# Moving filter sums, modulation loads and late adds in a fused FFT and FFN kernel

## The chip, the cores and the metric

The kernel runs on one core of one Trainium2 chip. The metric is device time in microseconds (us) of that core. It was 255.58 us before the change (median of 3 runs, 255.17 to 255.83).

The engines are named as in the profile: PE is the matmul engine, PEld its weight loads, DVE the vector engine, ACT the scalar engine, POOL the general engine (GpSimd), SP the engine that issues most of the DMAs. PSUM is the memory that matmuls write.

## The reference, cut to what matters

```python
def _A_ref(x, w_r, w_i):                      # x: (1, 2048, 640)
    X = rfft2(x.astype(float32))              # over both axes
    X = X * (w_r + 1j * w_i)                  # the "filter"
    return irfft2(X, s=(S, D)).astype(bfloat16)

def _B_ref(x, w_gate, w_up, w_down):          # 640 -> 1728 -> 640
    return silu(x @ w_gate) * (x @ w_up) @ w_down

mod = (silu(c) @ w_mod).reshape(1, 6, 1, -1)  # six vectors of 640
sa, ca, ga, sb, cb, gb = ...
h = layernorm(x) * (1 + ca) + sa
x = x + ga * _A_ref(h, A_w_r, A_w_i)
h = layernorm(x) * (1 + cb) + sb
x = x + gb * _B_ref(h, B_w_gate, B_w_up, B_w_down)
```

All inputs are bfloat16. Each FFT is done as a chain of matmuls with tables, so the program has four parts: a first DFT with layernorm statistics (0 to 37 us), a loop over 21 groups of columns that multiplies by the filter (37 to 62 us, its beginning is called the join here), the inverse DFT with the second layernorm (to 85 us), and the FFN in three chunks of rows (85 us to the end).

## The kernel before: the parts that matter

Everything large is loaded by one DMA queue, which SP issues. This is its order around the join. `Wn` holds the filter, `Wv` the filter in flipped row order, which the kernel first writes to device memory and then reads back. `wm_r[:, :, 0]` holds the gate weights (`ga`), `wm_r[:, :, 1:3]` those of `sb` and `cb`.

```python
for i, w in ((0, A_w_i), (2, A_w_r)):
    nc.sync.dma_start(Wn[:, i, :, :], w.rearrange(...)[:, :, 0:NW])        # filter
nc.sync.dma_start(KS2, K_dram[:, 384:576])
# ...
for i in range(2):
    nc.sync.dma_start(Wv[:, 2 * i, :, :], Wflip[i][:])                     # flipped filter
nc.sync.dma_start(Ktab[:, 0:384], K_dram[:, 0:384])
nc.sync.dma_start(wm_r[:, :, 0, :], wm_m[:, :, 0, :])                      # gate weights
# ... later, at the join:
t2_dma(0); t2_dma(1); t2_dma(2)                                            # DMA transposes
nc.sync.dma_start(wm_r[:, :, 1:3, :], wm_m[:, :, 1:3, :])                  # shift and scale weights
t2_dma(3)
```

The filter products need the sum of the real and imaginary filter. `wsum` makes it in pieces, on DVE or on POOL. The last three lines run just before the join.

```python
def wsum(W, lo, hi, eng):
    # ... views of columns lo to hi of the three filter planes
    eng.tensor_tensor(v[1], v[2], v[0], ALU.add)
# ...
if t == 13:
    wsum(Wn, 48, 64, nc.vector)          # 512 elements per partition
else:                                    # t == 15
    wsum(Wn, 0, 48, nc.vector)           # 1536 elements
    wsum(Wn, 64, 81, nc.gpsimd)
```

The group loop: `stage_a` is the matmul, `prod` the product on DVE. For the first two groups the second half of the product was put off. `ga_mod` makes the gate broadcast with matmuls, and the inner loop of `stage_a` makes the modulation columns.

```python
def stage_a(g):
    # ... for each column l of the group: a matmul, and at the first one:
        for c5 in {NG - 8: (0,), NG - 7: (0,), NG - 6: (1,), NG - 5: (1, 2), NG - 4: (2,), NG - 3: (3,), NG - 2: (3, 4), NG - 1: (4,)}.get(g, ()):
            # ... five small matmuls with wm_r[:, k, 1 + g % 2]
    prod(g, PP, xps, 0)
    if g > 1:
        prod(g, PP, xps, 1)
    return PP, xps
# ...
t2_pe(0)
wsum(Wv, 48, 64, nc.vector)
t2_pe(1)
PX = [stage_a(0)]
t2_pe(2)
PX.append(stage_a(1))
t2_pe(3)
ga_mod(0, 6)
ga_mod(320, 7, range(3))
for g in range(2):
    PPs[g] = PX[g][0]
    prod(g, *PX[g], 1)
for g in range(NG + 1):
    sa_add(g + 4 if g > 0 else 0)
    if g in (0, 1, 4):
        wsum(Wv, *{0: (64, 81), 1: (0, 16), 4: (16, 48)}[g], nc.gpsimd)
    if g + 2 < NG:
        PPs[g + 2] = stage_a(g + 2)[0]
    if g == 0:
        ga_mod(320, 7, range(3, NC5))
    # ...
```

Before the FFN the transposed rows come by DMA (`ln2_tr`), and `ln2_mod(0)` multiplies them in five pieces, all on POOL. In the FFN, `down_pair` is the down projection of two row tiles. It copies partial results out of PSUM on ACT and adds them on POOL. `a_sum` makes the sums of the Strassen-like scheme that the down projection uses.

```python
cps_ = [rL.cut((2560, 10496, 0, 1280)[i], [320], F32) for i in range(4)]
# ... in down_pair:
nc.scalar.copy(cps_[0], X)
nc.gpsimd.tensor_tensor(xa[:, 0:320], xa[:, 0:320], cps_[0], ALU.add)
# ...
nc.scalar.copy(cps_[2], X)                     # PE needs the PSUM bank of X again
nc.gpsimd.tensor_tensor(xb[:, 320:640], xb[:, 320:640], cps_[1], ALU.add)
nc.gpsimd.tensor_tensor(xa[:, 320:640], xa[:, 320:640], cps_[2], ALU.add)
# ... at the end of the last chunk:
r1, r2, r3, r4 = (lambda q=q: a_sum(ATc, 0, q, slice(0, 6)) for q in range(4))
```

The bytes of `cps_[2]` (0 to 1280 of `rL`) are also an input of a DVE product of the gate and up stage, line 1062.

## Time and profile before

| | before |
|---|---|
| time, median of 3 | 255.58 us |
| profiled span | 254.3 us |
| granted clock | 1.00 |
| PE, DVE, ACT, POOL busy | 245.3, 212.0, 162.3, 77.4 us |

These two lines of the page give the span and the busy time of each engine:

```profile
span 254.3 us, 6460 instructions
...
PE 245.3 (96%) x2513; PEld 200.1 (79%) x2513; DVE 212.0 (83%) x517; ACT 162.3 (64%) x299; POOL 77.4 (30%) x123
```

PE is busy for 96% of the span, so by the page's count a change of order alone can return at most its idle 9 us. The list of waits tells where they lie. Each line of it names an engine and line that waited, what released it, the total, how many waits, and the longest. These are the larger PE waits before, apart from one of 1.0 us at the very start:

```profile
PE psum L897 <- ACT rL L919: 0.8, 2, 0.4
PE psum L570 <- DMA rM<-in_w_mod_dram: 0.7, 1, 0.7
PE psum L566 <- DVE rM L541: 0.6, 1, 0.6
PE psum L971 <- POOL rW L784: 0.4, 1, 0.4
PE psum L537 <- ACT rA L403: 0.4, 1, 0.4
PE psum L897 <- DVE rE L854: 0.3, 1, 0.3
```

L537, L566 and L570 are the join and the group loop, L971 is the first matmul behind the second layernorm, and L897 is the down projection of the FFN. The DVE timeline at the join is next. Its columns are start, duration, engine, line, operation, and output and input with the shape per partition; a count above x1 joins neighbours.

```profile
36.61 1.90 DVE L410 TENSOR_TENSOR rW<-rW 128x1536 bf16<-128x1536 bf16 x1
38.43 0.47 DVE L541 TENSOR_TENSOR rM<-psum,gb_bc 128x256 bf16<-128x256 bf16 x2
38.83 0.41 DVE L410 TENSOR_TENSOR rW<-rW 128x512 bf16<-128x512 bf16 x1
39.34 2.06 DVE L588 TENSOR_TENSOR rM<-psum,rW 128x384 bf16<-128x384 f32 x4
```

DVE has no pause here. The long sum takes 1.90 us, more than four times the 0.41 us of a sum of a third of its size, and the first product starts at 39.34.

The wait at L919 reads as follows. ACT holds the copy back until DVE has finished L1062, which reads the bytes that the copy writes, and PE waits for the copy:

```profile
177.26 1.00 DVE L1062 TENSOR_TENSOR rX<-rH,rL 128x512 bf16<-128x512 bf16 x1
...
178.35 0.42 ACT L919 COPY rL<-psum 128x320 f32<-128x320 f32 x1 [1.39 <-DVE rX L1062]
...
178.83 1.11 PE L897 MATMUL psum<-rE 128*128 128x320 f16 x7 [0.42 <-ACT rL L919]
```

At the end of the last chunk DVE makes sums while POOL adds:

```profile
244.96 0.75 DVE L854 TENSOR_TENSOR rE<-rX 128x128 f16<-128x128 bf16 x1
245.63 0.68 DVE L856 TENSOR_TENSOR rE<-rE,rX 128x768 f16<-128x768 f16 x2
246.24 1.35 DVE L860 TENSOR_TENSOR rE<-rX,rE 128x768 f16<-128x768 bf16 x2
247.51 1.38 DVE L858 TENSOR_TENSOR rE<-rX 128x768 f16<-128x768 bf16 x2
...
244.77 0.86 POOL L910 TENSOR_TENSOR rM<-rM,rL 128x320 f32<-128x320 f32 x1 [17.83 <-ACT rL L909]
246.62 0.88 POOL L920 TENSOR_TENSOR rM<-rM,rL 128x320 f32<-128x320 f32 x1 [0.99 <-ACT rL L916]
247.95 0.86 POOL L921 TENSOR_TENSOR rM<-rM,rL 128x320 f32<-128x320 f32 x1 [0.45 <-ACT rL L919]
```

The two pairs that overlap a POOL add in full (L860 and L858) take twice as long as the pair that hardly does (L856).

### The profile page before, as it was taken

How to read it: one execution, taken by the hardware profiler on the slowest of the kernel's cores; microseconds unless marked ns; L12 is line 12 of the kernel's file. 1: busy time of each engine (PE TensorE's matmuls, PEld its weight loads, DVE VectorE, ACT ScalarE, POOL GpSimd, SP SyncE). 2: the span in 40 equal slices, each digit the busy share in tenths (PEclk: the TensorE clock that was granted, in tenths of full speed). 3: DMA queues.
4: the chain of work that ended last, by engine and by line, in shares of the span. 5: the costliest groups of instructions: out<-in, count | busy, mean ns of one | idle time of the engine just before them, and what ended most of it. 6: DMA issues, size and time to landing. Idle time of an engine off the chain costs nothing.

```text
span 254.3 us, 6460 instructions
## 1 busy us (share of the span) xinstructions
PE 245.3 (96%) x2513; PEld 200.1 (79%) x2513; DVE 212.0 (83%) x517; ACT 162.3 (64%) x299; POOL 77.4 (30%) x123
## 2 busy tenths in 40 slices
PE   8999998989999999999999999999999999999994
PEld 3678868989789888688877778886678887679962
DVE  2889898978898997779997997879985888993895
ACT  3678757978788686778862577674357765235630
POOL 7487785954022804000003900002220000440021
PEclk9999999999999999999999999999999999999999
DMA  6999999999999899600005020004210000211001
GB/s 220 396 348 298 283 391 175 264 314 389 283 350 269 198 263 172 142 14 0 3 0 106 17 76 15 3 3 80 70 44 14 3 0 17 39 52 54 4 0 52
DMA packets 45760, 34.43 MB, mean 135 GB/s; under 512 B 21731, under 2 KB 42658, under 8 KB 45346
## 3 DMA queue, kind: packets, MB, share of 16 engines
q1 hardware_dynamic: 43936, 30.00, 42.5%
q0 software_dynamic: 1504, 3.95, 6.6%
q8 instruction: 19, 0.31, 0.5%
q10 hardware_dynamic: 290, 0.08, 0.1%
q14 instruction: 11, 0.09, 0.1%
HBM read 26.72 MB, written 4.72 MB: 124 GB/s over the span
## 4 chain that ended last, share of the span: by engine, by line
PE 69%; DVE 10%; DMA 7%; issue 5%; POOL 4%; SPq 2%; ACT 2%; ACTq 0%; DVEq 0%; POOLq 0%
PE psum L1013 31%; PE psum L897 14%; PE psum L983 8%; DMA rM<-in_w_mod_dram 3%; PE psum L877 3%; SPq L518 2%; DMA rW<-rL 2%; DMA rE<-tab_R 2%; PE psum L971 2%; PE psum L595 2%; PE psum L397 1%; PE psum L396 1%; POOL rW L784 1%; PE psum L317 1%; PE psum L314 1%
## 5 line engine op out<-in xcount | busy, mean ns | idle before, releaser
L1013 PEld LDWEIGHTS <-rW 128*128 128x128 bf16 (+1 forms) x528 | 46.9, 98 | 5.6 <-issue 0.2
L910 POOL TENSOR_TENSOR rM<-rM,rL 128x320 f32<-128x320 f32 x7 | 7.0, 1002 | 85.9 <-ACT rL L909 85.9
L1013 PE MATMUL psum<-rW 128*128 128x256 bf16 (+1 forms) x240 | 27.1, 259 | 0.0
L897 PEld LDWEIGHTS <-rE 128*128 128x128 f16 (+1 forms) x196 | 18.8, 97 | 10.2 <-issue 1.2
L897 PE MATMUL psum<-rE 128*128 128x320 f16 (+1 forms) x147 | 22.7, 299 | 1.3 <-ACT rL L919 0.8
L1013 PE MATMUL psum<-rY,rW 128*128 128x256 bf16 (+1 forms) x96 | 24.0, 259 | 0.0
L983 PE MATMUL psum<-rW 128*128 128x256 bf16 (+1 forms) x170 | 23.1, 291 | 0.0
L588 DVE TENSOR_TENSOR rM<-psum,rW 128x384 bf16<-128x384 f32 (+2 forms) x42 | 20.2, 544 | 3.0 <-PE psum L566 2.5
L983 PEld LDWEIGHTS <-rW 128*128 128x128 bf16 x170 | 16.6, 98 | 3.8
L1013 PEld LDWEIGHTS <-rE 128*128 128x128 f16 x192 | 17.3, 98 | 2.6 <-DVE rE L961 0.3
L1049 DVE TENSOR_TENSOR rH<-psum,rW 128x512 bf16<-128x512 f32 x21 | 14.5, 689 | 5.8 <-PE psum L1013 3.9
L897 PEld LDWEIGHTS <-rX 128*128 128x128 bf16 (+1 forms) x151 | 14.6, 97 | 5.4
L758 POOL TENSOR_TENSOR rstd<-rstd,mhalf 128x4 f32<-128x4 f32 (+2 forms) x4 | 4.7, 1186 | 45.9 <-ACT rL L919 38.1
L1045 ACT COPY rH<-psum 128x512 f32<-128x512 f32 x21 | 12.3, 585 | 9.8 <-PE psum L1013 7.9
L1067 DVE TENSOR_TENSOR rX<-rH,rL 128x512 bf16<-128x512 bf16 x21 | 8.9, 424 | 9.9 <-ACT rL L1065 9.8
L1052 ACT COPY rX<-psum 128x512 f32<-128x512 f32 x21 | 12.3, 587 | 6.5 <-PE psum L1013 6.5
L1053 DVE TENSOR_TENSOR rX<-psum,rX 128x512 f32<-128x512 f32 x21 | 14.4, 685 | 2.1 <-ACT rX L1052 1.9
L1039 ACT COPY rW<-psum 128x512 f32<-128x512 f32 x21 | 12.3, 585 | 6.0 <-PE psum L1013 6.0
L385 DVE SCALAR_TENSOR_TENSOR rE<-rE,mv,psum 128x648 bf16<-128x648 f32 (+1 forms) x17 | 14.2, 845 | 1.9 <-PE psum L317 1.5
L897 PE MATMUL psum<-rA,rX 128*128 128x320 bf16 (+1 forms) x98 | 15.6, 299 | 0.0
L1013 PE MATMUL psum<-rH,rW 128*128 128x256 f16 (+1 forms) x96 | 15.1, 259 | 0.1
L1013 PE MATMUL psum<-rE,rY 128*128 128x256 f16 (+1 forms) x96 | 15.1, 259 | 0.0
(195 smaller groups left out, 679.9 us busy)
## 6 DMA issues: line engine op xcount, KB each, us to landing
out_dram<-rA SPq DMA_DIRECT2D x31, 80.0 KB, 1.6
rM<-in_w_mod_dram SPq DMA_DIRECT2D x3, 800.0 KB, 9.7
rX<-in_A_x_dram SPq DMA_DIRECT2D x3, 640.0 KB, 7.0
rA<-in_B_w_down_dram SPq DMA_DIRECT2D x2, 960.0 KB, 10.7
rM<-in_w_mod_dram SPq DMA_DIRECT2D x1, 1600.0 KB, 7.9
rY<-in_B_w_gate_dram POOLq DMA_DIRECT2D x2, 768.0 KB, 6.9
rW<-in_B_w_gate_dram SPq DMA_DIRECT2D x2, 640.0 KB, 7.3
rW<-in_B_w_up_dram SPq DMA_DIRECT2D x2, 640.0 KB, 7.6
```

What stands on the lines that cost most here:

```text
L385: nc.vector.scalar_tensor_tensor(Zv[:, h], Cv[:, h], mv[:, t, 0:1], zps[:, h], ALU.mult, ALU.subtract)
L588: nc.vector.tensor_tensor(PP[:, :, hl], xv[:, :, hl], in1, ALU.mult)
L877: nc.tensor.matmul(pop, lhsT=ATc[rows(k), k, tl * 128:(tl + 1) * 128], rhs=Wd_sb[rows(k), k, 320 * h:320 * h + 320], start=(k == 0), stop= ...
L897: nc.tensor.matmul(o, lhsT=lhsT, rhs=rhs, start=start, stop=stop, skip_group_check=True)
L983: nc.tensor.matmul(gu[u], lhsT=Wgu[:, u, c5, ff * 128:(ff + 1) * 128], rhs=h2T[:, :, c5, :], start=(c5 == 0), stop=(c5 == NC5 - 1))
L1013: nc.tensor.matmul(o[:, f], lhsT=w, rhs=b, start=(start and f == 0 and i == 0), stop=(stop and f == F - 1 and i == len(ops) - 1), skip_gro ...
L1039: nc.scalar.copy(c0, X)
L1045: nc.scalar.copy(c2, X)
L1049: nc.vector.tensor_tensor(c11, Z, c0, ALU.add)
L1052: nc.scalar.copy(c3, X)
L1053: nc.vector.tensor_tensor(c22, Y, c3, ALU.add)
L1067: nc.vector.tensor_tensor(ato, v4(c11), v4(g21), ALU.mult)
```

## The change

The change has five parts, and its intent is to close the PE waits listed above.

1. Start: the statistics are split, so that the first scale of POOL (`gscale(0)`) no longer stands behind the second tile's statistics. POOL's broadcast copy (`sc_rep`) and some warm-up matmuls (`idle_pe`) move too; the cut below leaves them out.
2. Join: the gate weights are loaded before the flipped filter, and their matmuls fill holes of PE. The POOL sum beside DVE's long sum goes away and comes back in small pieces later. The product of the first two groups is no longer split. The modulation columns come two groups later.
3. Before the FFN: one of the five pieces goes from POOL to ACT.
4. FFN: `cps_[2]` moves to bytes that L1062 does not read, and `h_sums` changes its order.
5. Tail: the last chunk's three adds go from POOL to DVE, and a third of its sums is made earlier.

```diff
+    nc.sync.dma_start(wm_r[:, :, 0, :], wm_m[:, :, 0, :])      # ahead of the flipped filter
     nc.sync.dma_start(KS2, K_dram[:, 384:576])
# ... start: stats(t) split into bn(t), gram_stats(t) and rstd_of(tiles)
+        gscale(0)
         t1(1)
-        stats(1)
-        gscale(0)
+        bn(1)
+        rstd_of((1,))
# ... join
                     wsum(Wn, 0, 48, nc.vector)
-                    wsum(Wn, 64, 81, nc.gpsimd)
# ...
-                    for c5 in {NG - 8: (0,), NG - 7: (0,), NG - 6: (1,), NG - 5: (1, 2), ...
+                    for c5 in {NG - 6: (0, 1), NG - 5: (0, 1), NG - 4: (2, 3), NG - 3: (2,), NG - 2: (4,), NG - 1: (3, 4)}.get(g, ()):
# ...
             prod(g, PP, xps, 0)
-            if g > 1:
-                prod(g, PP, xps, 1)
+            prod(g, PP, xps, 1)
# ...
+        ga_mod(320, 5, range(3))
         t2_pe(0)
         wsum(Wv, 48, 64, nc.vector)
         t2_pe(1)
-        PX = [stage_a(0)]
+        ga_mod(320, 5, range(3, NC5))
+        PPs[0] = stage_a(0)
         t2_pe(2)
-        PX.append(stage_a(1))
         t2_pe(3)
-        ga_mod(0, 6)
-        ga_mod(320, 7, range(3))
-        ...
+        wsum(Wn, 80, 81, nc.gpsimd)
+        wsum(Wv, 80, 81, nc.gpsimd)
+        PPs[1] = stage_a(1)
+        ga_mod(0, 6, range(2))
         for g in range(NG + 1):
-            if g in (0, 1, 4):
-                wsum(Wv, *{0: (64, 81), 1: (0, 16), 4: (16, 48)}[g], nc.gpsimd)
+            for W, lo, hi in {0: ((Wv, 0, 16),), 1: ((Wv, 16, 32),), 3: ((Wv, 32, 48),), 11: ((Wn, 64, 80),), 13: ((Wv, 64, 80),)}.get(g, ()):
+                wsum(W, lo, hi, nc.gpsimd)
# ... before the FFN
-            if ci == 0:
+            if ci == 0 and c5 < 4:
                 nc.gpsimd.tensor_scalar(h2T[:, :, c5, :], ...)
# ... FFN
-    cps_ = [rL.cut((2560, 10496, 0, 1280)[i], [320], F32) for i in range(4)]
+    cps_ = [rL.cut((2560, 10496, 9216, 1280)[i], [320], F32) for i in range(4)]
# ... tail (three adds, and the sums)
+        add = (nc.vector if last else nc.gpsimd).tensor_tensor
-        nc.gpsimd.tensor_tensor(xa[:, 0:320], xa[:, 0:320], cps_[0], ALU.add)
+        add(xa[:, 0:320], xa[:, 0:320], cps_[0], ALU.add)
# ...
+            if n == 2 and p == 2:
+                for q in (0, 2, 1, 3):
+                    a_sum(ATc, 0, q, slice(0, 2))
# ...
-            r1, r2, r3, r4 = (lambda q=q: a_sum(ATc, 0, q, slice(0, 6)) for q in range(4))
+            r1, r2, r3, r4 = (lambda q=q: a_sum(ATc, 0, q, slice(2, 6)) for q in range(4))
```

More of the change, by code (lines that the diff above doesn't have):

```diff
@@ L277, in adaln_block_kernel @@
         nc.sync.dma_start(Wn[:, i, :, :], w.rearrange("(k2 k1) l -> k1 k2 l", k1=P)[:, :, 0:NW])
+    wm_m = wm_v[:, :, 2 * D:6 * D].rearrange("p k (i d) -> p k i d", i=4)
+    nc.sync.dma_start(wm_r[:, :, 0, :], wm_m[:, :, 0, :])
     nc.sync.dma_start(KS2, K_dram[:, 384:576])
-    wm_m = wm_v[:, :, 2 * D:6 * D].rearrange("p k (i d) -> p k i d", i=4)
     nc.vector.memset(ones[:], 1.0)
@@ L296, in idle_pe @@
                              start=True, stop=True)
-    idle_pe(6)
+    idle_pe(4)
     def mod_cols(ps_ap, w_ap, ks=range(NC5), w=1):
@@ L338, in t1, with bn, rstd_of @@
             hTs[t] = hT
-        def stats(t):
-            if t in BN:
-                for k in range(2):
-                    nc.vector.bn_stats(bn6a[:, k, :], x_sb[:, t, 320 * k:320 * k + 320])
-                nc.vector.bn_aggr(mv[:, t, :], bn6a[:])
-            else:
-                gram_stats(t)
-            if t % 2 == 1 or t == 0:
-                us = (t,) if t < 2 else (t - 1, t)
-                for u in us:
-                    if u in BN:
-                        nc.vector.tensor_scalar(vtmp[:, u:u + 1], mv[:, u, 1:2], EPS, float(D), ALU.add, ALU.mult)
-                for tt in ([slice(t - 1, t + 1)] if t not in BN and t - 1 not in BN else [slice(u, u + 1) for u in us if u not in BN]):
-                    nc.vector.scalar_tensor_tensor(vtmp[:, tt], mv[:, tt, 0], -float(D), mv[:, tt, 0], ALU.mult, ALU.mult)
-                    nc.vector.scalar_tensor_tensor(vtmp[:, tt], ssq[:, tt], EPS * D, vtmp[:, tt], ALU.add, ALU.add)
-                tt = slice(us[0], t + 1)
-                nc.gpsimd.tensor_tensor(rstd[:, tt], vtmp[:, tt], mhalf[:, 0:len(us)], ALU.pow)
+        def bn(t):
+            for k in range(2):
+                nc.vector.bn_stats(bn6a[:, k, :], x_sb[:, t, 320 * k:320 * k + 320])
+            nc.vector.bn_aggr(mv[:, t, :], bn6a[:])
+        def rstd_of(us):
+            bns = [u for u in us if u in BN]
+            for u in bns:
+                nc.vector.tensor_scalar(vtmp[:, u:u + 1], mv[:, u, 1:2], EPS, float(D), ALU.add, ALU.mult)
+            for tt in ([slice(u, u + 1) for u in us if u not in BN] if bns else [slice(us[0], us[-1] + 1)]):
+                nc.vector.scalar_tensor_tensor(vtmp[:, tt], mv[:, tt, 0], -float(D), mv[:, tt, 0], ALU.mult, ALU.mult)
+                nc.vector.scalar_tensor_tensor(vtmp[:, tt], ssq[:, tt], EPS * D, vtmp[:, tt], ALU.add, ALU.add)
+            tt = slice(us[0], us[-1] + 1)
+            nc.gpsimd.tensor_tensor(rstd[:, tt], vtmp[:, tt], mhalf[:, 0:len(us)], ALU.pow)
         def gram_stats(t):
@@ L414, in adaln_block_kernel @@
             nc.tensor.matmul(cps[:, k:k + 1], lhsT=c_row[0:1, k * 128:(k + 1) * 128], rhs=one11[:], start=True, stop=True)
-        idle_pe(3)
+        idle_pe(4)
         nc.scalar.activation(sc_f[:], cps, ACT.Silu)
@@ L419, in adaln_block_kernel @@
                                 op=ALU.add)
+        bn(0)
         for r in range(4):
@@ L423, in adaln_block_kernel @@
         nc.gpsimd.memset(SAx[:], 0.0)
+        nc.gpsimd.tensor_copy(sc_rep[:], sc_f[:].unsqueeze(2).to_broadcast([P, NC5, 128]))
         flip_edge(A_w_i, Wflip[0])
@@ L428, in adaln_block_kernel @@
         nc.sync.dma_start(Ktab[:, 0:384], K_dram[:, 0:384])
-        nc.sync.dma_start(wm_r[:, :, 0, :], wm_m[:, :, 0, :])
+        rstd_of((0,))
         t1(0)
-        stats(0)
         idle_pe(1)
@@ L457, in adaln_block_kernel @@
         gscale(1)
-        nc.gpsimd.tensor_copy(sc_rep[:], sc_f[:].unsqueeze(2).to_broadcast([P, NC5, 128]))
         t1(3)
-        stats(2)
+        gram_stats(2)
         zout(1)
@@ L463, in adaln_block_kernel @@
         t1(4)
-        stats(3)
+        gram_stats(3)
+        rstd_of((2, 3))
         dfwd(2)
@@ L471, in adaln_block_kernel @@
                 t1(t + 3)
-            if t + 2 < NT:
-                stats(t + 2)
+            u = t + 2
+            if u < NT:
+                (bn if u in BN else gram_stats)(u)
+                if u % 2:
+                    rstd_of((u - 1, u))
             if t > 3:
@@ L567, in stage_a @@
                 if i == 0:
-                    for c5 in {NG - 8: (0,), NG - 7: (0,), NG - 6: (1,), NG - 5: (1, 2), NG - 4: (2,), NG - 3: (3,), NG - 2: (3, 4), NG - 1: (4,)}.get(g, ()):
+                    for c5 in {NG - 6: (0, 1), NG - 5: (0, 1), NG - 4: (2, 3), NG - 3: (2,), NG - 2: (4,), NG - 1: (3, 4)}.get(g, ()):
                         for k in range(NC5):
@@ L574, in stage_a @@
             prod(g, PP, xps, 0)
-            if g > 1:
-                prod(g, PP, xps, 1)
-            return PP, xps
+            prod(g, PP, xps, 1)
+            return PP
         def prod(g, PP, xps, hl):
@@ L676, in adaln_block_kernel @@
         t2_pe(1)
-        PX = [stage_a(0)]
+        ga_mod(320, 5, range(3, NC5))
+        PPs[0] = stage_a(0)
         t2_pe(2)
-        PX.append(stage_a(1))
         t2_pe(3)
-        ga_mod(0, 6)
-        ga_mod(320, 7, range(3))
-        for g in range(2):
-            PPs[g] = PX[g][0]
-            prod(g, *PX[g], 1)
+        wsum(Wn, 80, 81, nc.gpsimd)
+        wsum(Wv, 80, 81, nc.gpsimd)
+        PPs[1] = stage_a(1)
+        ga_mod(0, 6, range(2))
         for g in range(NG + 1):
             sa_add(g + 4 if g > 0 else 0)
-            if g in (0, 1, 4):
-                wsum(Wv, *{0: (64, 81), 1: (0, 16), 4: (16, 48)}[g], nc.gpsimd)
+            for W, lo, hi in {0: ((Wv, 0, 16),), 1: ((Wv, 16, 32),), 3: ((Wv, 32, 48),), 11: ((Wn, 64, 80),), 13: ((Wv, 64, 80),)}.get(g, ()):
+                wsum(W, lo, hi, nc.gpsimd)
             if g + 2 < NG:
-                PPs[g + 2] = stage_a(g + 2)[0]
+                PPs[g + 2] = stage_a(g + 2)
             if g == 0:
-                ga_mod(320, 7, range(3, NC5))
+                ga_mod(0, 6, range(2, NC5))
             if g == NG - 3:
@@ L778, in ln2_tr, with ln2_mod @@
             xn2c[:, 0:n].rearrange("p tl (c q) -> p (tl c) q", c=NC5))
-    def ln2_mod(ci):
+    def ln2_mod(ci, cs=range(NC5)):
         h2T = h2T_of(ci)
-        for c5 in range(NC5):
-            if ci == 0:
+        for c5 in cs:
+            if ci == 0 and c5 < 4:
                 nc.gpsimd.tensor_scalar(h2T[:, :, c5, :], h2T[:, :, c5, :], one_p_cb[:, c5:c5 + 1], modcols[:, 2, c5:c5 + 1],
                                         ALU.mult, ALU.add)
-            elif c5 % 2 == 0 or ci > 1:
+            elif ci and c5 % 2 == 0 or ci > 1:
                 nc.vector.tensor_scalar(h2T[:, :, c5, :], h2T[:, :, c5, :], one_p_cb[:, c5:c5 + 1], modcols[:, 2, c5:c5 + 1],
@@ L919, in down_pair @@
         nc.scalar.copy(cps_[2], X)
-        nc.gpsimd.tensor_tensor(xb[:, 320:640], xb[:, 320:640], cps_[1], ALU.add)
-        nc.gpsimd.tensor_tensor(xa[:, 320:640], xa[:, 320:640], cps_[2], ALU.add)
+        add(xb[:, 320:640], xb[:, 320:640], cps_[1], ALU.add)
+        add(xa[:, 320:640], xa[:, 320:640], cps_[2], ALU.add)
         if not last:
@@ L957, in h_sums @@
         tt(t1, b11, b12, ALU.subtract)
-        tt(t3, b22, b12, ALU.subtract)
         tt(t2, b22, t1, ALU.add)
@@ L961, in h_sums @@
         nc.vector.tensor_scalar_mul(t2, t2, -1.0)
+        tt(t3, b22, b12, ALU.subtract)
     def h_neg(ci):
@@ L1164, in adaln_block_kernel @@
                 ln2_sq(2 + (5,7,9,11).index(t))
-            if t == 10:
-                ln2_mod(0)
+            if t in (10, 13):
+                ln2_mod(0, range(4) if t == 10 else range(4, 5))
             if t == 14:
```

## The prediction

> **What bounds it now.** One core, granted clock 1.00 throughout, span 254.3 us. The busy table has the tensor engine (PE) at 245.3 us, VectorE (DVE) at 212.0, so no change of order can return more than about 9 us of PE idle time. The list of waits and the timeline place that idle time: start-up 0-15 us (about 1.5 us, of which 1.0 can't be had), the join between the two FFT stages at 37-40 us (0.36 on the last eviction, 0.6 on DVE), 0.7 at 52.2 us on the DMA of the modulation weights, 0.39 at 84.4 us on POOL's last modulation piece, 2 x 0.42 at 178 and 219 us on the ScalarE copy L919, and about 3.8 after 243 us.
>
> **Start.** POOL's gscale(0) stands behind the second rstd (9.94) and makes the first s1 wait 0.4 us; one_p_ca sits behind bn_stats on DVE. Moving both up should give PE about 0.5 us.
>
> **Join.** The removed POOL sum overlapped DVE's 1536-element sum, which took 1.90 us; from the 0.42 us of the 512-element ones I estimate 1.1 alone. The skill agrees ("GPSIMD Engine Reference", Specifications: SBUF interfaces are shared with VectorE, contention with instructions of two SBUF inputs). DVE is 100% busy from 36.6 to 50 us, so this looks like 0.7 us. But the DMA queue was full until 40 us and landed in order: filter 32.3, flipped filters 34.9 and 37.55, table 37.9, gate weights 40.0. Issuing the gate weights (0.8 MB, 2.1 us) first pushes the second flipped filter to about 39.7. DVE needs it for its 48-64 sum before its first product; that sum ran at 38.8. So first products start later (39.34 before, 40.1-40.6 after), DVE waits about 1.3 us on that DMA, and the start-up gain is swallowed there. In return: the holes of 0.29 and 0.34 us among the first products close, gate matmuls fill the 0.36, and the modulation columns (two groups later, first needed near 54.5, landing 52.9) stop costing 0.7. Start, join and filter loop together: only 0.5 us (-0.5 to 1.8).
>
> **84 us.** Four pieces on POOL, the fifth on ScalarE: 0.35 us.
>
> **FFN.** cps_[2] leaves the bytes that L1062 reads, so L919 no longer waits 1.4 us for DVE; PE, which is bound there, gets 2 x 0.42 = 0.8 us.
>
> **Tail.** DVE's sums run 243.9-248.9. A third of them moves to idle DVE time near 238.5, and the POOL adds (0.86 each), beside which these sums took 0.7-0.75 us per pair instead of about 0.5, become three DVE adds of about 0.42 after the sums. The sums should end near 246.6, and PE is then bound: 1.1 us.
>
> **Sum.** 0.5 + 0.35 + 0.8 + 1.1 = 2.8 us: 252.7 us, 8 in 10 between 251.0 and 254.2. Chances: faster by over 2% (below 250.5) 0.09, within 2% 0.90, slower by over 2% 0.01.
>
> **What would show it.** Start: s1(0) without a wait. Join: a DVE (or PE) wait of about 1 us before the Wv sum on DMA rW<-wflip_r, landing 39.3-40; the long sum near 1.1 us; no wait at L570. 84 us: wait under 0.1. FFN: no PE wait on L919. Tail: no POOL instruction after 244 us; last matmul about 4.2 us after 245.5 in the shifted clock, that is, about 1 us earlier relative to the chunk's start.
>
> **What would make it wrong.** If the flipped filters land as before, the join alone gives 0.8 us more. If POOL's remaining sums, now beside DVE's 48-64 sum, slow it to 1 us, the join loses. Late modulation columns, two in most of the last six groups, can make PE the limit there. The ScalarE piece may delay the last eviction before the FFN.

## The result, and the profile after

| | before | after |
|---|---|---|
| time, median of 6 each | 255.71 us (255.17 to 256.67) | 252.12 us (251.68 to 252.60) |
| ratio, 95% interval | | 0.9858, 0.9835 to 0.9880 |
| profiled span | 254.3 us | 250.8 us |
| mean granted clock | 1.000 | 0.999 |

A ratio is the mean time of one kernel's fast runs over that of the other's fast runs of the same rounds, so it is not quite the ratio of the medians quoted. The change gains 1.4%. A later set of the same kernel gave 0.9911 (run e12 below). The page of the changed kernel has this line:

```profile
PE 243.4 (97%) x2512; PEld 200.1 (80%) x2512; DVE 210.1 (84%) x524; ACT 163.1 (65%) x300; POOL 74.4 (30%) x122
```

By this count PE's idle time fell only from 9.0 to 7.4 us (span less busy), while the span fell by 3.5. The rest lay in time that the page counts as busy, so the 9 us were not a firm bound; e1 below shows how part of a hole gets counted as busy.

The time divides well at a few instructions that every version has. In the next table, T1 is the first PE transpose of the join, C the copy of the modulation columns behind the last filter product, F the first FFN matmul, and D the first matmul of the last two row tiles' down projection. All are read from the timelines of one profile each. The last column is a second profile of the changed kernel, taken in a later set (run e12 below).

| stretch | before | after | difference | after again (e12) |
|---|---|---|---|---|
| start to T1 | 37.55 | 37.16 | -0.39 | 36.52 |
| T1 to C (join and group loop) | 24.81 | 24.14 | -0.67 | 26.95 |
| C to F | 22.72 | 22.68 | -0.04 | 22.20 |
| F to D (most of the FFN) | 157.77 | 156.51 | -1.26 | 156.49 |
| D to the end (tail) | 11.45 | 10.31 | -1.14 | 10.34 |
| span | 254.3 | 250.8 | -3.5 | 252.5 |

The two lower stretches repeat to 0.03 us. Those before the FFN do not, and most of the experiments are about them. These are the PE waits after, complete but for two of 0.2 us, and the DVE wait that is new:

```profile
PE psum L296 <- DVE warm L285: 1.0, 1, 1.0
PE psum L567 <- DVE rM L588: 1.0, 1, 1.0
PE psum L335 <- DMA rX<-in_A_x_dram: 0.7, 1, 0.7
PE psum L972 <- POOL rW L784: 0.3, 1, 0.3
...
DVE rW L407 <- DMA rW<-wflip_r: 1.1, 1, 1.1
```

(Most line numbers have moved a little: L566 is now L567, L537 L538, L971 L972, L410 L407. The wait of 1.0 at L296 belongs to the start-up and stood in the profile before too.) The waits on L919, on the modulation weights at L570 and on the tail sum L854 are gone. A wait of PE on the first product (L588) and one of DVE on the flipped filter are new. The join on DVE:

```profile
36.22 0.95 DVE L407 TENSOR_TENSOR rW<-rW 128x1536 bf16<-128x1536 bf16 x1
37.65 0.49 DVE L542 TENSOR_TENSOR rM<-psum,gb_bc 128x256 bf16<-128x256 bf16 x2 [0.48 <-ACT rA L400]
39.27 0.43 DVE L407 TENSOR_TENSOR rW<-rW 128x512 bf16<-128x512 bf16 x1 [1.13 <-DMA rW<-wflip_r]
39.62 2.87 DVE L588 TENSOR_TENSOR rM<-psum,rW 128x384 bf16<-128x384 f32 x6
```

The long sum takes half of its time, 0.95 us. Still the first product starts at 39.62, later than the 39.34 of before, because the sum ahead of it waits for the flipped filter. The tail on DVE:

```profile
242.47 0.23 DVE L854 TENSOR_TENSOR rE<-rX 128x128 f16<-128x128 bf16 x1
242.61 0.56 DVE L856 TENSOR_TENSOR rE<-rE,rX 128x512 f16<-128x512 f16 x2
...
243.55 0.55 DVE L858 TENSOR_TENSOR rE<-rX 128x512 f16<-128x512 bf16 x2
244.02 0.48 DVE L911 TENSOR_TENSOR rM<-rM,rL 128x320 f32<-128x320 f32 x1
```

The small sum takes 0.23 us instead of 0.75. The sums end at 244.10, which is 3.61 us after D (240.49); before it was 6.04 us after D (248.89 less 242.85). PE has no listed wait in the whole stretch after D.

### The profile page after: what moved, and what is told of

Read it like the earlier page. It is cut to its first block, busy times and chain, and to the rows that moved or that the text cites. A ratio compares the mean times of both kernels' runs of the same rounds, so it can differ in the third digit from the quotient of the medians.

```text
span 250.8 us, 6472 instructions
## 1 busy us (share of the span) xinstructions
PE 243.4 (97%) x2512; PEld 200.1 (80%) x2512; DVE 210.1 (84%) x524; ACT 163.1 (65%) x300; POOL 74.4 (30%) x122
## 4 chain that ended last, share of the span: by engine, by line
PE 68%; DMA 12%; SPq 9%; issue 4%; DVE 2%; POOL 2%; ACT 0%; DVEq 0%; POOLq 0%; ACTq 0%
PE psum L1014 32%; PE psum L897 19%; PE psum L984 9%; DMA rM<-rA 4%; DMA rW<-wflip_r 4%; PE psum L877 3%; DMA rW<-rL 3%; SPq L273 2%; SPq L277 2%; DMA rM<-in_w_mod_dram 2%; SPq L275 2%; PE psum L972 2%; SPq L279 2%; PE psum L595 1%; PE psum L567 1%
## 5 line engine op out<-in xcount | busy, mean ns | idle before, releaser
L911 POOL TENSOR_TENSOR rM<-rM,rL 128x320 f32<-128x320 f32 x6 | 5.9, 976 | 68.3 <-ACT rL L910 68.3
L897 PEld LDWEIGHTS <-rE 128*128 128x128 f16 (+1 forms) x196 | 19.1, 97 | 7.7
L897 PE MATMUL psum<-rE 128*128 128x320 f16 (+1 forms) x147 | 22.3, 299 | 0.0
L588 DVE TENSOR_TENSOR rM<-psum,rW 128x384 bf16<-128x384 f32 (+2 forms) x42 | 20.0, 541 | 1.8 <-PE psum L567 0.9
L897 PEld LDWEIGHTS <-rX 128*128 128x128 bf16 (+1 forms) x151 | 14.6, 97 | 5.4
L897 PE MATMUL psum<-rA,rX 128*128 128x320 bf16 (+1 forms) x98 | 15.6, 299 | 0.0
```

The lines of the kernel that those rows point to most:

```text
L588: nc.vector.tensor_tensor(PP[:, :, hl], xv[:, :, hl], in1, ALU.mult)
L897: nc.tensor.matmul(o, lhsT=lhsT, rhs=rhs, start=start, stop=stop, skip_group_check=True)
```

## The experiments

The theory behind the prediction was that four terms are simple (start, modulation piece, copy target, tail), and that the join returns little because the flipped filter lands later. The rivals were that the join's gain comes from the end of contention with POOL, that the copy target is only one of several releasers of that PE wait, and that the tail's gain belongs to one of its two parts alone. Twelve versions ran, in four sets on three chips; e12 is the changed kernel itself. All gave correct results. Where the edit says "on before" it was made to the old kernel, otherwise to the new one.

### e1: the copy target alone, on before

```diff
-    cps_ = [rL.cut((2560, 10496, 0, 1280)[i], [320], F32) for i in range(4)]
+    cps_ = [rL.cut((2560, 10496, 9216, 1280)[i], [320], F32) for i in range(4)]
```

> The kernel before with one line changed: the third ScalarE copy of each down pair gets its own bytes (offset 9216). Theory: both waits of PE on that copy (0.42 us each as listed; 0.57 us each from start to start of the matmuls) go, PE is bound there and nothing else takes over: 1.1 us less, 254.6 us against 255.7, and the 98 matmuls of the pair stretch take 13.4 us instead of 13.9. Rival: DVE, which does its sums there beside POOL's adds, becomes the limit and gives back half: at most 0.5 us less, with a new PE wait on a DVE sum.

Measured: 254.88 us (254.07 to 255.10, 4 runs), ratio 0.9971 (0.9939 to 1.0003). The stretch from F to D went from 157.77 to 156.59 us, that is -1.18. The ACT and PE lines that stood at 178 us now read:

```profile
177.32 0.43 ACT L919 COPY rL<-psum 128x320 f32<-128x320 f32 x1 [0.53 <-PE psum L897]
...
178.02 1.12 PE L897 MATMUL psum<-rE 128*128 128x320 f16 x7
```

The interval of the total includes 1, so the total by itself shows no gain; the stretch does, in one profile of each. What follows: the copy is released by PE itself, and the PE wait is gone in both chunks. The two stretches that hold it became shorter by 0.57 and 0.59 us, while each listed wait was 0.42. The listed wait is too small because the modelled record of a matmul lasts 0.30 us, while the next of a train starts 0.136 us after it (seven matmuls of L897 end 1.12 us after the first starts, so (1.12 - 0.30) / 6); the idle time is counted only from the end of that record. So 0.8 us was really 1.16. The rest of the -1.26 of the whole change, 0.1 us, lies where `h_sums` was reordered (not run apart, so that it is the cause is not shown): the stretch between the first two chunks' down projections took 40.42 us before, 40.41 in e1 and 40.29 after.

### e2: the gate weights in their old place

```diff
-    nc.sync.dma_start(wm_r[:, :, 0, :], wm_m[:, :, 0, :])     # ahead of the flipped filter
+    (the same load behind Ktab, as before)
-        ga_mod(320, 5, range(3)) ... ga_mod(320, 5, range(3, NC5)) ... ga_mod(0, 6, range(2))
+        ga_mod(0, 6)                     # both before the loop, as before
+        ga_mod(320, 7, range(3))
```

> The kernel after, with the gate weights' load back behind the flipped filters and the gate matmuls back behind the four PE transposes. Theory: the early gate weights are what delays the second flipped filter. It should land near 37.4 instead of 39.2 us, DVE's wait for it should vanish, the first product should start near 38.6 instead of 39.6 us; PE gets the 0.4 us hole before the transposes back and the gate matmuls wait until about 39.5. Products are then 0.3 to 0.6 us earlier until the last transposed columns, which the DMA brings at 54.6 to 55.9 us, hold PE: total 0 to 0.5 us less than after. Rival: the fill of the join is what pays, and undoing it costs 0.5 us or more.

Measured: 252.46 us (252.05 to 253.23, 4 runs), ratio 0.9885 (0.9858 to 0.9912). The first product started at 37.70 us instead of 39.62, without a wait, so the landing of the flipped filter was what held it. Of these 1.9 us only 0.5 were left at C (60.80 instead of 61.30): PE waited 0.9 us for the gate weights, which now landed at 39.5, and DVE stood still for 1.46 us at 41.1. At F nothing was left, and e2 was even 0.63 us later (84.61 instead of 83.98): the DMA transpose was issued 0.5 us earlier but landed 0.5 us later (81.1 instead of 80.6), and the four POOL pieces started only then:

```profile
81.26 2.53 POOL L783 TENSOR_SCALAR rW<-rW,one_p_cb,modcols 128x256 bf16<-128x256 bf16 x4 [8.79 <-DMA rW<-rL]
...
82.73 0.27 PE L971 MATMUL psum<-rW,Wp 128*128 128x256 bf16 x1 [0.54 <-POOL rW L783]
...
83.85 0.38 PE L971 MATMUL psum<-rW,Wp 128*128 128x256 bf16 x2 [0.31 <-POOL rW L783]
```

What follows: a gain at the join is worth something only if the next DMA landings come earlier too. Here the next landing took back all of it and more.

### e3: the start as before

```diff
-        bn(0) and rstd_of((0,)) ahead of t1(0); gscale(0) ahead of t1(1)
+        the old order: t1(0), then statistics of 0; gscale(0) behind statistics of 1
# also back: the warm-up matmuls (idle_pe) and POOL's broadcast copy (sc_rep)
```

> The kernel after with the order of the start as before (statistics of tile 0, its scaled table, warm-up matmuls, the broadcast copy). Theory: PE ends the first FFT stage 0.4 us later, but the wait of DVE for the second flipped filter shrinks from 1.1 to about 0.7 us, the first product stays at 39.6 us, and the total stays within 0.2 us of after. Rival: the whole 0.4 us comes through to the end.

Measured: 252.81 us (251.44 to 254.54, 4 runs), ratio 0.9899 (0.9849 to 0.9949). This run by itself is inconclusive for 0.5 us: its four times spread over 3.1 us, and its profile had a DVE wait of 2.7 us on the flipped filter and a fall of the clock, of which more below. What can be said comes from T1 in all fourteen profiles: the five with the old start (before, e1, e3, e5, e6) have T1 at 36.83 to 37.55, mean 37.20, and the nine with the new start at 36.29 to 37.16, mean 36.64. The difference is 0.56 us. Across chips the two ranges overlap; within each set they don't (e1 and e3 37.07 and 36.83, against e2 and e4 36.29 and 36.52; e5 and e6 37.17 and 37.39, against e7 and e9 36.97 and 36.56).

The traces also show where it arises. "The first s1" of the prediction is four matmuls of PE that start at 11.14, 11.60, 11.75 and 11.89 us before, and at 10.95, 11.09, 11.23 and 11.37 after. In the old order the first two wait for POOL's two instructions of `gscale(0)`. From the start of the matmul ahead of them to the start of the fourth it takes 1.03 to 1.05 us in all five profiles with the old start, and 0.48 in all nine with the new one. So PE gains about 0.55 us there, as predicted. How much of it reaches the end is not shown.

### e4: the POOL sum beside DVE's long sum again

```diff
                     wsum(Wn, 0, 48, nc.vector)
+                    wsum(Wn, 64, 81, nc.gpsimd)      # and the later pieces 80:81 and 64:80 of Wn removed
```

> The kernel after with POOL's filter sum of columns 64 to 80 put back beside DVE's sum of 48 columns. Theory: that DVE sum goes from 0.95 to 1.7 to 1.9 us, as before, but DVE waits for the flipped filter afterwards anyway; the first product stays at 39.6 us (at most 0.1 later) and the total within 0.2 us of after. Rival: the contention was on the critical path and the total rises by 0.7 us.

Measured: 252.00 us (251.31 to 253.05, 4 runs), ratio 0.9867 (0.9832 to 0.9902), within the interval of the change itself. DVE's sum was back at 1.91 us. The wait for the flipped filter behind it was still 0.54 us, although the filter landed 0.85 us earlier in this profile (38.3), and the first product started at 38.77. What follows: the contention is real (0.95 against 1.91 us for the same sum), but in the new order it is paid out of a wait for a DMA. Ending it gained nothing that these runs can show.

### e5 and e6: the two parts of the tail, each alone on before

```diff
# e5
+        add = (nc.vector if last else nc.gpsimd).tensor_tensor        # and the three adds through it
# e6
+            if n == 2 and p == 2:
+                for q in (0, 2, 1, 3):
+                    a_sum(ATc, 0, q, slice(0, 2))                     # and slice(2, 6) later
```

> The kernel before with only the three adds of the last down pair moved from POOL to DVE. Measure: from the first matmul of the last down pair to the end of the span, 11.45 us before, 10.3 after. Theory: the POOL adds slow DVE's 16-bit sums beside them; without them the sums (0.75, 1.35 and 1.38 us) take about 0.25, 0.7 and 0.7 us, and this stretch falls by about 0.75 us to 10.7. Rival: the three adds only change engines, DVE becomes longer by 1.2 us, and the stretch stays or grows.

> The kernel before with only a third of the last chunk's sums done early, the adds still on POOL. Theory: four sums get shorter by about 0.13 us each, but POOL still slows them, so the stretch from the first matmul of the last down pair to the end falls by 0.3 to 0.5 us from 11.45 us. Rival: the early sums are the main part and give 0.8 us or more.

Measured in one look each: the stretch from D to the end took 10.65 us in e5 and 10.88 in e6, against 11.45 before and 10.31 with both. So the adds gave 0.80 us (0.75 was expected), the earlier sums 0.57 (0.3 to 0.5 was expected), and both together 1.14, which is less than the 1.37 of their sum. The totals, 256.13 and 255.89 us, are single runs of unknown state and are not compared. The DVE sums of e5 and then those of e6, which answer to the lines of before:

```profile
245.86 0.23 DVE L854 TENSOR_TENSOR rE<-rX 128x128 f16<-128x128 bf16 x1
...
246.60 0.69 DVE L860 TENSOR_TENSOR rE<-rX,rE 128x768 f16<-128x768 bf16 x2
247.21 0.69 DVE L858 TENSOR_TENSOR rE<-rX 128x768 f16<-128x768 bf16 x2
```

```profile
245.20 0.89 DVE L854 TENSOR_TENSOR rE<-rX 128x128 f16<-128x128 bf16 x1
...
246.95 1.21 DVE L858 TENSOR_TENSOR rE<-rX 128x512 f16<-128x512 bf16 x2
```

What follows: without POOL beside it, a pair of 768 takes 0.69 us instead of 1.35 to 1.38. With POOL beside it, the small sum still takes 0.89 us and the last pair 1.21 in e6. Both parts are needed.

### e7: all five modulation pieces on POOL again

```diff
-            if ci == 0 and c5 < 4:
+            if ci == 0:
```

> The kernel after with all five modulation pieces of the first FFN chunk on POOL again. Theory: the DMA transpose lands at about the same time whatever PE gained before (80.8 us after, 81.2 before), so the five pieces end 3.2 us later, PE waits about 0.9 us where it waits 0.3 in after, and the FFN starts 0.6 us later: from POOL's first piece to the first FFN matmul 3.85 us, as before, against 3.2 in after; total 0.4 to 0.6 us more than after. Rival: ScalarE's piece gave next to nothing, since the listed wait went only from 0.39 to 0.32 us: under 0.15 us.

Measured: 253.41 us (252.94 to 254.75, 4 runs), ratio 0.9904 (0.9870 to 0.9938). In its profile and in that of the changed kernel PE comes to this place at the same time (82.41), and POOL begins its pieces at the same time (80.78 and 80.76). F is 84.42 here and 83.98 there. So the piece on ACT is worth 0.44 us where PE comes early enough to be bound by it. The profiled span is worse by more than that (251.9 against 250.8 us), and the extra 0.7 us of this pair has a separate cause, which is the next point. Whether it also explains the other runs of e7 is not shown, for they have no profile.

### A throw of the dice in the first chunk

In every profile the stretch between the first two chunks' down projections takes either 40.28 to 40.42 us (before, after, e1, e2, e3, e4, e10, e12, e13) or 41.00 to 41.21 (e5, e6, e7, e9, e11). No edit of e5, e6 or e7 touches it. These are DVE and POOL in the changed kernel, then in e7:

```profile
138.84 0.61 DVE L854 TENSOR_TENSOR rE<-rX 128x896 f16<-128x896 bf16 x1
...
138.86 1.31 POOL L921 TENSOR_TENSOR rM<-rM,rL 128x320 f32<-128x320 f32 x1
```

```profile
139.28 1.36 DVE L854 TENSOR_TENSOR rE<-rX 128x896 f16<-128x896 bf16 x1
...
139.30 0.85 POOL L921 TENSOR_TENSOR rM<-rM,rL 128x320 f32<-128x320 f32 x1
```

The two instructions start within 0.02 us of each other. Either DVE's sum takes 0.61 us and POOL's add 1.31, or DVE's takes 1.36 and POOL's 0.85. All nine profiles of the first group have the first form and all five of the second group have the second. The Trainium skill, "SBUF — State Buffer", section "SBUF: two separate sides", says that DVE and GpSimd share a pair of ports as an exclusive lock, and that whichever starts first has it for the whole instruction while the other blocks. The trace agrees in part: the loser takes its own time and most, but not all, of the winner's (1.36 is 0.61 and 0.75; 1.31 is 0.85 and 0.46). Which of them wins can't be read from the trace: DVE's start is recorded 0.02 us before POOL's in all fourteen profiles, also in the five in which POOL keeps its 0.85. The second form goes with 0.7 to 0.8 us more in this stretch, with no edit at fault. So e5, e6, e7 and e9 could not be read from the span of their one profile, and were read by stretch.

### e9: the modulation columns two groups earlier, as before

```diff
-                    for c5 in {NG - 6: (0, 1), NG - 5: (0, 1), NG - 4: (2, 3), ...
+                    for c5 in {NG - 8: (0,), NG - 7: (0,), NG - 6: (1,), ...
```

> The kernel after with the modulation columns two groups earlier again, as in before. Theory: PE reaches them near 51.5 us, their weights land near 52.6, so the wait of PE on that DMA comes back with about 1 us; part is given back because the columns no longer crowd the last six groups and the hole at 56 us on the last transposed columns closes, and part because the DMA transpose before the FFN lands no later: last product 0.3 to 0.7 us later, total 0 to 0.5 us more than after. Rival: the full 0.9 us to the end.

Measured: 253.17 us (252.31 to 253.69, 4 runs), ratio 0.9879 (0.9848 to 0.9911). The wait on the modulation weights was back:

```profile
PE psum L571 <- DMA rM<-in_w_mod_dram: 0.9, 1, 0.9
```

C was 61.80 instead of 61.30, but F was 83.97 and so the same as with the columns late (83.98), because the transpose before the FFN landed at 80.4, and at 80.6 with the columns late. What follows: the later columns gain 0.5 us at C, and in these two profiles nothing at F. It is the second case, after e2, in which the next landing takes a gain back.

### e10 and e11: half of the down weights behind the transpose, alone and with e2

```diff
-    for h in range(2):
+    def load_wd(h):
         nc.sync.dma_start(Wd_sb[:, HK * h:HK * h + 6, :], ...)
+    load_wd(0)
# ...
                 ln2_tr(0)
+                load_wd(1)
```

> The kernel after with half of the down projection's weights (0.96 MB) issued behind the first chunk's DMA transpose instead of before it. Theory: that transpose waits in a full DMA queue, so with 0.96 MB less ahead of it it lands 2 to 3 us earlier, at 78 to 79 us; POOL's pieces are done before PE comes, the PE wait of 0.3 us there is gone, and what the first stages gain comes through: 0.3 to 0.6 us less than after. Rival: the transpose takes its 6 to 7 us by itself, lands where it did, and nothing changes; or DVE's folding of the late weights holds PE in the first chunk and it is slower.

> e2 (gate weights late again) together with e10. Theory: e2 had its last product 0.5 us earlier than after and lost it to PE's waits on the modulation pieces (1.1 us in its profile), because the DMA transpose landed no earlier. With the queue shortened these waits go: 0.3 to 0.8 us less than e10 alone if the start is equal. Rival: e2's order of the join is simply no better, and it is within 0.2 us of e10.

If the transpose before the FFN is late because 0.96 MB of down weights stand in the queue ahead of it, moving them should free what e2 gained. Measured: e10 253.99 us (252.47 to 254.99, 6 runs), ratio 0.9933 (0.9898 to 0.9968); e11 252.76 us (251.50 to 254.35, 6 runs), ratio 0.9891 (0.9857 to 0.9926). The transpose did land earlier, at 78.2 and 77.9 us instead of 80.6, and PE no longer waited for it. But the gate and up weights, next in the queue, came later, and PE waited for those. This is e11:

```profile
PE psum L985 <- DMA rW<-in_B_w_up_dram: 1.6, 1, 1.6
```

In e10 the wait was 0.35 us. What follows: the first half of the expectation held and the second half did not. On the pages of e10 and e11 the DMA engines are 80% busy or more in every slice from 6 to 100 us, and the wait only changed its place. The Trainium skill, "DMA: Bandwidth & Descriptors", section "Queues, rings and completion order", says that each DMA engine takes the descriptors of one queue in order. In these traces the loads of the SP queue did land in the order of issue: before, flipped filter 34.9 and 37.6, table 37.8, gate weights 40.0; after, gate weights 33.7, flipped filter 36.3 and 39.2, table 39.4.

### e12: the changed kernel once more, in the rounds of e10 and e11

> The kernel after once more, in the same rounds as e10 and e11, and as a second profile: the ratio to before should be 0.986 within 0.002. Its profile shows which of the times of after move from run to run: the landing of the second flipped filter and of the DMA transposes by up to 1 us, the stretches bound by PE by less than 0.05 us.

Measured: 253.89 us (251.51 to 254.28, 6 runs), ratio 0.9911 (0.9877 to 0.9946). The first set had 0.9858 (0.9835 to 0.9880), so the expectation of 0.986 within 0.002 failed, while the stretches from F on repeated to 0.03 us as expected. The same kernel is 1.8 us slower here, and its runs spread over 2.8 us; 11 runs of before in the same rounds spread over 1.8 us with a median of 255.66. Its profile shows a slow case. First DVE's wait and PE's idle time, then the windows; the windows' columns are busy time of PE, PEld, DVE, ACT and POOL with the number of instructions, granted clock, DMA share and GB/s.

```profile
40.45 0.42 DVE L407 TENSOR_TENSOR rW<-rW 128x512 bf16<-128x512 bf16 x1 [2.95 <-DMA rW<-wflip_r]
...
41.85 0.80 PE L567 MATMUL psum<-Ktab,rM 128*128 128x192 bf16 x4 [2.80 <-DVE rM L588]
```

```profile
38.00:42.00 4.00, 1.20 (x17) 0.95 (x14) 1.55 (x4) 1.38 (x3) 2.43 (x7) 0.88 1.18 136
42.00:44.00 2.00, 2.00 (x15) 1.60 (x14) 1.71 (x4) 0.42 (x1) 1.27 (x3) 0.50 1.25 274
44.00:46.00 2.00, 1.95 (x27) 1.80 (x26) 1.18 (x3) 1.29 (x3) 1.29 (x2) 0.88 0.81 158
```

The flipped filter landed at about 40.4 us instead of 39.2. PE then stood idle for 2.8 us, and its granted clock fell to 0.50 (it was 1.00 from 36 to 38 and from 46 to 50): narrower windows put the fall at 41.1 us, 2.0 us after the last matmul's end, and the rise at 44.5. A train of four matmuls took 0.80 us, and 0.49 in the first profile. So the filter that came 1.2 us later delayed C by 2.17 us (63.47 instead of 61.30). e3 showed the same (idle 2.6 us, clock 0.50, first product 40.86, C 63.71). In e7, by contrast, the filter landed at 39.4, PE stood idle for 1.4 us, the clock stayed at 1.00, and C was 61.30. The Trainium skill, "TensorE: Matmul & The Clock Gate", section "What's actually happening", gives half speed for an idle matmul engine after a window of about 3.4 us. The trace agrees in kind; here a listed idle time of 2.6 to 2.8 us was enough, and the half speed lasted 3.4 us.

The mean clock marks such runs without a profile: three of the six runs of e12 have 0.993 (254.28, 253.82 and 253.96 us), as has the profiled run of e3 (254.54) and one of e7 (254.75). No run of before has it; its lowest is 0.997. All five are among the 34 runs of versions that load the gate weights early (after, e3, e4, e7, e9, e10, e12), and none is among the 16 with the load late (e2, e11, e13); that is too few to prove a link. It isn't the only cause of slow runs, for one run of e12 with a clock of 0.999 took 254.19 us, and three of e10 with 0.997 to 1.000 took 254.53 to 254.99.

### e13: the gate weights late, their matmuls spread, the pieces shared by three engines

```diff
# e2's place for the gate load, and
-        ga_mod(320, 5, range(3)) ... (all gate matmuls at the join)
+            if g in (1, 2):
+                ga_mod(320 * (g - 1), 5 + g)          # inside the group loop
# ln2_mod(0): two pieces on POOL, two on DVE, one on ACT
-            if ci == 0 and c5 < 4:
+            if ci == 0 and c5 < 2:
-            elif ci and c5 % 2 == 0 or ci > 1:
+            elif (c5 % 2 == 0 if ci else c5 < 4) or ci > 1:
```

> An attempt at a better version: e2 (gate weights late) with the gate matmuls moved behind the second and third group of the loop, so that PE doesn't wait for their weights before it feeds DVE, and the modulation pieces of the first chunk spread over three engines (two on POOL, two on DVE, one on ScalarE), since the DMA transpose lands near 81 us whatever came before. Theory: first product near 38 us, DVE's hole of 1.1 to 1.5 us among the first products closes to 0.4 or less, last product 0.3 to 0.9 us earlier than e2, PE waits at the FFN's start 0.2 to 0.6 instead of 1.1 us; no hole of PE over 1.5 us in the join, so the granted clock stays 1.00 there in every run, and the runs scatter no more than those of before. Total 251.0 to 252.2 us where before is 255.7, ratio 0.982 to 0.986, better than after in the rounds of e12 (0.991). Rival: the loop is held by the last transposed columns (54 to 56 us) and the FFN's start by its weights, and it is no better than e2 (0.9885).

Measured: 251.72 us (251.34 to 252.22, 6 runs), ratio 0.9846 (0.9822 to 0.9869), span 249.5 us. It answers to both losses of e2: the gate matmuls run after their weights have landed, and the pieces before the FFN take less time behind the transpose. These are POOL and PE before the FFN, where the remaining PE wait is 0.17 us:

```profile
80.01 1.10 POOL L781 TENSOR_SCALAR rW<-rW,one_p_cb,modcols 128x256 bf16<-128x256 bf16 x2 [8.19 <-DMA rW<-rL]
...
81.94 0.38 PE L969 MATMUL psum<-rW,Wp 128*128 128x256 bf16 x2 [0.17 <-DVE rW L784]
```

The first product starts at 37.83, C is 60.15 and F is 82.70, that is 1.15 and 1.28 us earlier than in the first profile of the changed kernel. From POOL's first piece to F it takes 2.69 us, and 3.22 there. It is 1.5% below the kernel before. Against the changed kernel, the set of e12 on the same chip gives means of 253.47 and 251.72 us, and the two intervals against before do not overlap; against that kernel's first set (0.9835 to 0.9880) they do. Its six runs spread over 0.9 us, those of e12 over 2.8, and none of its runs has a clock below 0.997. But the first set of the changed kernel also spread over 0.9 us, and e13 ran in later rounds than e12, so that it is faster or steadier than the changed kernel is not shown. Its two edits were not run apart.

## Why the prediction was right or wrong

The total was right: 252.7 us predicted, 252.12 measured, in the range. The second set's 253.89 is in the range too. That the sum came so near is partly luck. In the first pair of profiles the first term was 0.56 us too small, the second 0.31 too large and the third 0.46 too small, and the two sets gained 3.6 and 1.8 us, on either side of 2.8. The terms fared as follows.

| term | predicted | measured | verdict |
|---|---|---|---|
| start, join and loop together | 0.5 | 1.06 in the first profile, -1.11 in e12's | mechanism right, size not fixed |
| before the FFN | 0.35 | 0.04 (C to F), listed wait 0.39 to 0.32 | wrong as a saving |
| FFN | 0.8 | 1.26, of which the copy target 1.18 (e1) | right cause, too small |
| tail | 1.1 | 1.14 | right |
| sum | 2.8 | 3.5 in spans of the first pair, 3.6 and 1.8 in the two sets' medians | right |

**Start.** "Moving both up should give PE about 0.5 us" was right: the first s1 took 0.55 us less in every profile with the new start, and the means of T1 differ by 0.56 (see e3). But the new order met another wait in the first profile, 0.66 us on the x load at 8 us, and how much of the gain reaches the end was not measured.

**Join.** "So first products start later (39.34 before, 40.1-40.6 after)" was right in kind. They started at 39.62 in the first profile and at 40.79 in e12's, with waits of 1.13 and 2.95 us on the DMA of the flipped filter; the prediction said 1.3 and a landing near 39.7, and it was 39.2 and 40.4. e2 shows that the moved gate load is the cause: with it back, the products started at 37.70. The long sum took 0.95 us where 1.1 was estimated. The page "GPSIMD Engine Reference", Specifications, on which that estimate leaned, agrees with the trace. e4 shows that ending this contention is worth nothing here, as the prediction said it would look like more than it is. The fear that POOL's new pieces would slow the 48-64 sum didn't come true (0.43 us). What failed is the size, "only 0.5 us": one number was put on a sum that differs by 2.17 us between two profiles of the same kernel. The range named was -0.5 to 1.8, and e12's profile is below it. The step that the prediction lacked is the fall of PE's clock in its longer idle time, as e12 and e3 show it.

**Before the FFN.** "Four pieces on POOL, the fifth on ScalarE: 0.35 us" was the step that failed, and "wait under 0.1" with it. The wait was 0.32 us. POOL could start its first piece only 0.45 us earlier (80.76 instead of 81.21), while PE arrived 1.03 us earlier (82.41 instead of 83.44), so PE ate the saving by arriving early. The piece on ACT does its work, 0.44 us by e7, but it came out as a part of the join's gain being kept, not as a gain on top of it.

**FFN.** "PE, which is bound there, gets 2 x 0.42 = 0.8 us" had the right mechanism: e1 alone removed both waits. The size was read from listed waits, which leave out about 0.15 us for each hole. The missing terms are 2 x 0.15 for that and 0.1 in the stretch where `h_sums` was reordered.

**Tail.** "The sums should end near 246.6, and PE is then bound: 1.1 us" was right. In the clock of before that is 3.75 us after D, and 3.61 was measured. The adds took 0.48 us each on DVE, and no POOL instruction ran there.

What stays open: why the same queue brings the flipped filter at 38.3 us in one profile (e4) and at 40.4 in another (e12, e3), of which only half is seen (it was issued at 29.03 us in e4 and at 30.07 and 30.05 in e12 and e3, and took 9.3, 10.3 and 10.4 us from there; SP spent 3.35 us on issuing the gate load in e4, and 4.66 and 4.52 in e12 and e3); what made the 254.19 us run of e12 slow at full clock; and how much of the start's 0.55 us reaches the end.

## What to carry to other kernels

Treat a listed PE wait as a lower bound, and check every saving ahead of a DMA landing against that landing: here the 1.9 us of e2 shrank to 0.5 at C, and neither that nor the 0.5 us of the later columns (e9) was left at F. Before a load is moved up in a full queue, see what it pushes back and who waits for that; in two profiles here (e12, e3) a wait of 2.6 to 2.8 us on the matmul engine cost more than its length, for its clock fell to half. Compare versions by stretches between fixed instructions and by several runs, for here the order of two instructions that start 0.02 us apart on DVE and POOL went with 0.7 us of a single span.

## What the Trainium skill lacked or had wrong

- "TensorE: Matmul & The Clock Gate" gives half speed after at least one idle window of about 3.4 us. Here less than that was enough: a listed idle time of 2.6 us (e3) and 2.8 us (e12) lowered the granted clock to 0.50, in e12 already 2.0 us after the last matmul's end, and one of 1.5 us (e10) did not. The half speed lasted about 3.4 us (2 us in full, and shares of 0.88 in 4 and 2 us on both sides: 0.96 and 0.48 us). The listed time leaves out about 0.15 us of each hole.
- No page that I read says by how much a listed matmul wait falls short of the hole: 0.42 us was listed and 0.57 to 0.59 came back (e1), because the modelled record of 0.30 us outlasts the start of the next matmul, 0.136 us later.
- "GPSIMD Engine Reference" names the contention with VectorE without a size in time. Here a 16-bit sum of two inputs took 0.95 us alone and 1.90 to 1.91 beside POOL, and a pair of sums of 768 took 0.69 and 1.35 to 1.38.
- "SBUF — State Buffer" has the exclusive lock, and says that the loser blocks fully. Here the loser lost 0.75 of the winner's 0.85 us, or 0.46 of 0.61. It lacks what follows when both start within 0.02 us: DVE's sum took 0.61 or 1.36 us, with the same recorded order of starts, and the stretch around it moved by 0.7 to 0.8 us from profile to profile.
- "DMA: Bandwidth & Descriptors" has the order of a queue, but nothing on how much a landing varies. The same load of 1 MB in the same queue took 9.3, 9.6 and 10.3 us from issue to landing in three profiles (e4, after, e12), and landed at 38.3, 39.2 and 40.4 us.
